# Another program order, other buffer slots and some exchanged engines in a fused linear-attention and FFN kernel

## Chip, cores and metric

The kernel runs on one core of a Trainium2 chip. The metric is the device time of one execution in microseconds (us). The engines are TensorE (PE in the profile, its weight loads PEld), VectorE (DVE), ScalarE (ACT), GpSimd (POOL) and SyncE (SP), which issues nearly all DMAs.

## What is computed

The reference is an attention with sketched polynomial features, without softmax, followed by a multiplicative feed-forward network (FFN).

```python
batch, n_heads, seq, head_dim, r = 4, 4, 1088, 32, 8
def phi(x):                       # 64 features per token and head
    a = np.einsum('rd,bhsd->bhsr', S1, x)
    b = np.einsum('rd,bhsd->bhsr', S2, x)
    return np.einsum('bhsi,bhsj->bhsij', a, b).reshape(*x.shape[:-1], r * r)
q_p, k_p = phi(q), phi(k)
kv  = np.einsum('bhsf,bhsd->bhfd', k_p, v)
z   = np.sum(k_p, axis=2)
num = np.einsum('bhsf,bhfd->bhsd', q_p, kv)
den = np.einsum('bhsf,bhf->bhs', q_p, z)[..., None] + 1e-06
x   = (num / den).transpose(0, 2, 1, 3).reshape(4352, 128)
out = (((x @ w1) * (x @ w2)) @ w3) @ w_out        # d_ff 1024, back to 128
```

S1, S2 and the FFN weights arrive as float64, so the kernel converts their raw words to float32 itself.

## The kernel before

The program is a list of 1179 named steps. Each step is a small function that issues one or a few instructions; the string `ORDER` says in which order the steps are called, and every engine then works its own instructions off in that order, since the kernel chains each engine's instructions (the loop at its end). So what stands in front of an instruction on its engine is decided by `ORDER` alone, and an instruction that waits holds up all that stands behind it on that engine.

Three other tables belong to it. `SLOTS` gives, for each kind of tile, which buffer the next tile of that kind takes, in the order of the calls (kind `b` is the 8 PSUM banks). `POOL` names the steps that run on GpSimd and not on VectorE (`on`), `CPV` the copies that run on VectorE and not on ScalarE (`cp`). At most four bulk loads (`UNDER_WAY`) are in flight.

The names of the steps:

- `s.*` prepares the sketch matrices; `warm0` to `warm11` are fillers, matmuls on zeros into an unused tile (`idle_ps`, L255).
- `k0` to `k3` are the key blocks, one for each batch: lead and rest split the keys (`rest0` is L651 on VectorE), `gram0` to `gram4` (L659) are gram matmuls of the splits (`ps_g`), G, T and N an orthonormalisation in small tiles, `kp` the features, `kv` their product with v.
- `q0` to `q7` and `qr` are the query parts: products with the small matrices (`ps_a`, `ps_c`), split and corrected values (`s_g`, `s_hl`, `ay_C`), `dn`, `de`, `rc` the denominator, `phi` features, `x` the result in PSUM; `xT` (L1291 for the first part) is the FFN's input with its rows on partitions.
- `w*` load and convert the weights; `f*` fold w3 and w_out into one matrix `w3o`.
- `g0` to `g3` are the FFN of the first four groups of 512 tokens, done directly: `a` (L1799) and `b` (L1809) are matmuls of 512 columns, `c` copies one result to SBUF, `m` multiplies them (L1815), `o` is the output matmul (L1835). `gr` is the same for the remaining 256 tokens, in 256 columns, with `o` at L1824.
- `h4` and `h6` treat the last four groups in two pairs, with seven products in place of eight: first-layer matmuls on 64 rows of the array at L1673 (two run side by side), elementwise combinations `m` and `T` (L1707 to L1742, 128x512), second-layer matmuls `P` of 64 columns (L1759, side by side too), combinations `k1` to `k9` (L1767 to L1785).
- `oT` transposes a group's output (L1842), `oS` scales it (L1848, GpSimd; it needs `q4.ns` or `q6.ns`, 16 small copies at L1497 that lay out the factors), `st` stores it with four DMAs (L1556), and `gr.st1` (L1562) is the last store.

So the program falls into a start (loads, sketches, first key block, first query part), a long part in which FFN matmuls of g0 to g3 alternate with the attention of the other blocks, the two seven-product stages, and a tail.

## Time and profile before

| | |
|---|---|
| three runs | 244.77, 245.26, 245.58 us; median 245.26 |
| profiled execution: span | 244.1 us from first to last instruction |
| mean granted TensorE clock | 0.998 |
| HBM read and written | 19.40 and 2.23 MB |

The page cuts the span into 40 slices and gives the busy tenths of each engine:

```profile
PE   8998999899999999999999999999999999999994
DVE  2876988999899998997899878498989789999792
POOL 4576658344856998764583889929999425883670
DMA  7959797078859897200000000360000000000054
```

In the list of costly groups a row names the line, the engine, the operation, the tiles and shapes, then the sum of busy time and the mean of one, then the idle time in front of them. In a timeline a row is start, duration, engine, line, tiles; several alike that run close together are merged (x4), so its duration reaches from the first start to the last end. Matmuls overlap, and so their pitch is read from their starts. A wait row gives the sum, the count and the longest.

### The profile page before, as it was taken

Reading aid. Unit: us, or ns where it says so; the run is one execution under the profiler, and the core shown is the slowest. Engines: PE = TensorE matmul, PEld = TensorE weight load, DVE = VectorE, ACT = ScalarE, POOL = GpSimd, SP = SyncE. Lnnn points to the kernel's source line nnn. Section 1 sums busy time; section 2 is a strip of 40 time slices with the busy share of each in tenths; the row PEclk is TensorE's granted clock in tenths of the full one; section 3 lists DMA queues with packets and bytes.
Section 4 is the critical chain, followed back from the end, with each engine's and each line's share of the span. In section 5 each row is a group of like instructions: output and inputs, shape, how many; then the busy total and the mean of one; then the engine's idle time right before and its main releaser. Section 6 shows DMA issues by size and latency. Waiting matters only on the chain.

```text
span 244.1 us, 6745 instructions
## 1 busy us (share of the span) xinstructions
PE 236.2 (97%) x2724; PEld 129.8 (53%) x2724; DVE 206.7 (85%) x421; ACT 123.5 (51%) x246; POOL 161.9 (66%) x203
## 2 busy tenths in 40 slices
PE   8998999899999999999999999999999999999994
PEld 5887454545545646766566444444443354463363
DVE  2876988999899998997899878498989789999792
ACT  3976957675666764593012914355651164730010
POOL 4576658344856998764583889929999425883670
PEclk9999999999999999999999999999999999999999
DMA  7959797078859897200000000360000000000054
GB/s 201 265 143 325 181 227 190 6 197 224 220 141 251 188 217 190 59 1 3 3 0 0 4 0 3 59 113 3 1 0 0 0 3 0 0 1 3 12 90 93
DMA packets 31935, 22.06 MB, mean 90 GB/s; under 512 B 21280, under 2 KB 26528, under 8 KB 31904
## 3 DMA queue, kind: packets, MB, share of 16 engines
q1 hardware_dynamic: 31360, 21.11, 35.1%
q8 instruction: 21, 0.34, 0.6%
q10 hardware_dynamic: 544, 0.52, 0.6%
q14 instruction: 10, 0.08, 0.1%
HBM read 19.40 MB, written 2.23 MB: 89 GB/s over the span
## 4 chain that ended last, share of the span: by engine, by line
PE 87%; DMA 5%; ACT 2%; POOL 2%; DVE 1%; issue 1%; POOLq 0%; SPq 0%
PE b_ps L1809 12%; PE ps_o L1835 12%; PE ps_X L1673 11%; PE a_ps L1799 11%; PE ps_o L1759 10%; PE ps_w3o L534 6%; PE ps_Y L1673 6%; PE ps_Z L1673 3%; PE ps_g L659 2%; PE ps_x L1527 2%; PE ps_ac L1374 2%; DMA qh<-in_q_dram 2%; DMA k<-in_k_dram 2%; PE ps_or L1824 2%; POOL ph L1208 1%; PE idle_ps L255 1%
## 5 line engine op out<-in xcount | busy, mean ns | idle before, releaser
L1673 PE MATMUL ps_X<-xd,wv 64*128 64x512 f32 x112 | 36.3, 593 | 0.0
L1799 PE MATMUL a_ps<-xT,w 128*128 128x512 f32 (+1 forms) x80 | 36.1, 562 | 0.0
L1809 PE MATMUL b_ps<-xT,w 128*128 128x512 f32 (+1 forms) x80 | 35.6, 555 | 0.0
L1804 ACT COPY ffa<-a_ps 128x512 f32<-128x512 f32 (+1 forms) x38 | 20.1, 540 | 29.2 <-PE a_ps L1799 26.7
L1707 POOL TENSOR_TENSOR hc<-hc 128x512 f32<-128x512 f32 x16 | 20.7, 1304 | 15.7 <-DVE hc L1685 15.5
L1835 PE MATMUL ps_o<-ab,w3o 128*128 128x512 f32 x64 | 29.6, 600 | 0.0
L1680 ACT COPY hc<-ps_X 128x512 f32<-128x512 f32 x38 | 21.3, 590 | 16.1 <-PE ps_X L1673 12.9
L1815 DVE TENSOR_TENSOR ab<-ffa,b_ps 128x512 f32<-128x512 f32 (+1 forms) x40 | 23.9, 623 | 4.9 <-PE b_ps L1809 4.1
L501 POOL TENSOR_TENSOR w3c<-w3c,cv_m 128x512 int32<-128x512 int32 x16 | 21.2, 1344 | 4.2 <-DVE w3c L495 4.1
L1673 PEld LDWEIGHTS ps_X<-xd,wv 64*128 64x128 f32 x112 | 14.9, 186 | 13.1 <-issue 10.9
L1799 PEld LDWEIGHTS a_ps<-xT,w 128*128 128x128 f32 x80 | 14.1, 189 | 13.9 <-issue 8.8
L1809 PEld LDWEIGHTS b_ps<-xT,w 128*128 128x128 f32 x80 | 14.4, 190 | 13.1 <-issue 8.1
L1673 PE MATMUL ps_Y<-xd,wv 64*128 64x512 f32 x48 | 19.7, 594 | 0.0
L1835 PEld LDWEIGHTS ps_o<-ab,w3o 128*128 128x128 f32 x64 | 11.6, 190 | 13.4 <-issue 13.0
L534 PEld LDWEIGHTS ps_w3o<-wo,w3T 128*128 128x128 f32 x128 | 15.3, 192 | 2.4 <-issue 2.4
L534 PE MATMUL ps_w3o<-wo,w3T 128*128 128x128 f32 x128 | 15.7, 276 | 0.0
L1759 PE MATMUL ps_o<-hc,w3o 128*64 128x512 f32 x32 | 15.1, 595 | 0.0
L1759 PE MATMUL ps_o<-tt,ws 128*64 128x512 f32 x32 | 13.7, 594 | 0.0
L1680 ACT COPY hc<-ps_Y 128x512 f32<-128x512 f32 x14 | 8.1, 592 | 9.7 <-PE ps_Y L1673 6.6
L263 ACT ACTIVATE cv_c<-raw 128x1024 f32<-128x1024 f32 (+1 forms) x13 | 13.0, 1014 | 0.0
L1540 ACT COPY xd<-ps_x 64x256 f32<-64x256 f32 x24 | 8.8, 367 | 7.2 <-PE ps_o L1835 6.8
L1497 POOL COPY nz<-nz 32x8 f32<-32x8 f32 x32 | 11.1, 347 | 1.4
(347 smaller groups left out, 593.0 us busy)
## 6 DMA issues: line engine op xcount, KB each, us to landing
raw<-in_moe_w_dram SPq DMA_DIRECT2D x32, 256.0 KB, 5.0
qh<-in_q_dram SPq DMA_DIRECT2D x4, 544.0 KB, 4.5
raw<-in_moe_w_dram SPq DMA_DIRECT2D x4, 512.0 KB, 5.8
out_dram<-oT SPq DMA_DIRECT2D x32, 64.0 KB, 2.0
k<-in_k_dram SPq DMA_DIRECT2D x3, 512.0 KB, 5.1
v<-in_v_dram SPq DMA_DIRECT2D x2, 512.0 KB, 6.1
kh<-in_k_dram SPq DMA_DIRECT2D x8, 128.0 KB, 3.6
raw<-in_moe_w_out_dram SPq DMA_DIRECT2D x4, 256.0 KB, 5.0
```

The costliest lines, as they stand in the source:

```text
L263: act.activation(dst, hi.bitcast(F32), ACT.Prelu, scale=2.0 ** -112, alpha=-2.0 ** 32)
L501: pool.tensor_tensor(d, d, x["m"][:, i * 512:(i + 1) * 512], ALU.add)
L534: pe.matmul(t["o"], w3T[ko][:, c], wo[:, c], start=c == 0, stop=c == NC - 1)
L1673: pe.matmul(x[bank], stat(j, u)[:, i * 128:(i + 1) * 128], rows(j, u), start=new, stop=True, tile_position=(u * 64, 0), skip_group_check=True)
L1680: cp(n(y))(x[k], x[bank])
L1707: on(f"h{g}.{i}m{k}").tensor_mul(both[0][k], both[0][k], both[1][k])
L1759: pe.matmul(acc_o[bank][half[0]:half[1]], w(i), x(i), start=n == 1, stop=n == (2 if j == 3 else 4), tile_position=(0, half[0]), skip_group ...
L1799: pe.matmul(x["a"][:, :w], w_of(0, c), xT[g][:, c0:c0 + w], start=True, stop=True)
L1804: cp(f"g{g}.{c}{su}c")(x["s"][:, :w], x["a"][:, :w])
L1809: pe.matmul(x["b"][:, :w], w_of(1, c), xT[g][:, c0:c0 + w], start=True, stop=True)
L1815: dve.tensor_mul(ab_sb[g, c][:, c0:c0 + w], x["s"][:, :w], x["b"][:, :w])
L1835: pe.matmul(o_ps[g], w3o[:, c], ab_sb[g, c], start=n == 1, stop=n == NC)
```

## The change

The file's functions stay as they are; four tables differ. The first 60 steps of `ORDER` are the same and the rest is permuted. `SLOTS` gives other buffers to the tiles. 26 steps leave `POOL` and 34 enter it; 14 copies leave `CPV` and 16 enter it. A line or two of each table:

```diff
 SLOTS = {
     "b": 
-        "012345670214657210671306537457462512346127340273014526045721472352140327540542370673245716"
+        "012345670214567201570316245173056437605247134671352075241304675326530012653074265304361427"
...
-    "x": "012012201110",
+    "x": "012012021020",
 }
...
 POOL = set("""
-    g4.oS g5.oS g6.oS g7.oS h4.0T1 h4.0T2 h4.0T3 h4.0m12 h4.0m22 h4.1T2 h4.1m11 h4.1m12 h4.2m11
+    g4.oS g5.oS g6.oS g7.oS h4.0T1 h4.0T2 h4.0T3 h4.0T4 h4.0m11 h4.0m12 h4.0m22 h4.1T1 h4.1T2 h4.1T3
...
 CPV = set("""
-    g0.0c g0.1c h4.1ac h4.1ad h6.1bc h6.2ad k0.kT1 k1.kvc k2.kT1 k2.kq k3.kT0 k3.kT1 k3.kq q0.xc0
-    q0.xc1 q6.xT0 q6.xT2
+    g0.6c g1.1c g2.3c g2.6c gr.3c h4.0ae h4.1ac h4.1bc h4.2ae h4.3ac h4.3ai h6.1ac h6.2ac h6.k1
+    k0.kT1 k0.kz q0.xc1 q4.xT3 q6.xT1
...
 ORDER = """
...
-g4.oS h6.k2 h6.k4 h6.0P3 gr.7o0 g4.st gr.0a gr.5b h6.k5 h6.k6 h6.3P3 h6.1P3 h6.k7 g5.oS q6.ns gr.4a gr.3o0 gr.4b gr.0c
...
+h6.2P7 gr.1m h6.0T4 g5.oT h6.3P1 h6.1P6 q6.ns h6.3P7 gr.3m h6.k1 h6.2P6 h6.2P4 h6.3P2 h6.k2 h6.0P7 h6.3P6 h6.3P5
...
```

Of the 128x512 products of the two seven-product stages, 16 go from VectorE to GpSimd and 7 from GpSimd to VectorE. The steps that an engine does at three places follow, before and now.

TensorE where the first FFN matmuls begin; `ps_xs` leads to xT, `ps_ab` belongs to the second key block, `ps_g` is its gram. Before:

```order
L1287 MATMUL ps_xs<-ident,xs 128x128 x2
L727 MATMUL ps_ab<-kT,KS 32x128 x16
L1799 MATMUL a_ps<-xT,w_81 128x512 x2
L1809 MATMUL b_ps<-xT,w_81 128x512 x2
L1799 MATMUL a_ps<-xT,w_81 128x512
L659 MATMUL ps_g<-kk 32x64
L659 MATMUL ps_g<-k,kk 32x32
```

Now:

```order
L829 MATMUL ps_krab<-RS,krT 128x64
L805 MATMUL ps_kq<-ident,kvc 128x128 x2
L727 MATMUL ps_ab<-kT,KS 32x128 x16
L1267 MATMUL ps_xt<-pT,kz_634 64x256 x4
L1287 MATMUL ps_xs<-ident,xs 128x128 x4
L659 MATMUL ps_g<-kk 32x64
L659 MATMUL ps_g<-k,kk 32x32
```

The gram rows go on in this way for 48 matmuls (gram0 to gram2); only then come L1809 and L1799. The query matmuls L1110, which stood between two parts of L1287 just ahead of these rows, are further ahead.

VectorE ahead of the first xT. `s_g`, `s_t`, `s_hl` and `ay_C` are of the second query part, `s_loy`, `s_pr`, `s_d`, `s_rc` of the first, and `kk` (L651) is rest0 of the second key block. Before:

```order
L1198 RECIPROCAL s_rc<-s_rc 128x16
L466 TENSOR_SCALAR w_81<-cv_c 128x2x256
L1274 COPY xc<-ps_xt 128x256 x2
L1291 TENSOR_TENSOR xT<-xc,ps_xs 128x256 x2
L1137 TENSOR_REDUCE s_g<-ps_a 128x32
L201 SCALAR_TENSOR_TENSOR s_t_699<-s_g,ps_a 128x256
L1130 STREAM_TRANSPOSE ay_C<-ps_c 128x384
L204 SCALAR_TENSOR_TENSOR s_hl<-s_g,s_t_699 128x2x128
L1157 TENSOR_TENSOR s_hl<-ps_a,s_hl 128x2x128
L651 TENSOR_TENSOR kk<-k,kk 128x1152
```

Now:

```order
L1101 TENSOR_TENSOR s_loy<-s_loy,ay_C_592 128x128
L1130 STREAM_TRANSPOSE ay_C<-ps_c 128x384
L1176 TENSOR_TENSOR s_pr<-s_hla,s_hiy 128x256
L204 SCALAR_TENSOR_TENSOR s_hl<-s_g,s_t_595 128x2x128
L794 COPY kz_634<-ps_kz 128x128
L1157 TENSOR_TENSOR s_hl<-ps_a,s_hl 128x2x128
L1189 TENSOR_REDUCE s_d<-s_pr 128x2x16
L1194 SCALAR_TENSOR_TENSOR s_rc<-s_d 128x16
L1198 RECIPROCAL s_rc<-s_rc 128x16
L651 TENSOR_TENSOR kk<-k,kk 128x1152
L1274 COPY xc<-ps_xt 128x256
L1291 TENSOR_TENSOR xT<-xc,ps_xs 128x256 x2
```

The steps of the second query part and L651 stood behind L1291 and stand now ahead of it; one of the two copies L1274 and the weight shift L466 are gone from here.

GpSimd at the end. `hc` and `tt` are the products of the last stage, `nz` the factors (`q6.ns`), `oT` the groups' outputs. Before:

```order
L1732 TENSOR_TENSOR tt<-hc,tt 128x512
L1707 TENSOR_TENSOR hc<-hc 128x512
L1727 TENSOR_TENSOR tt<-hc 128x512
L1737 TENSOR_TENSOR hc<-hc 128x512
L1742 TENSOR_TENSOR tt<-tt,hc 128x512
L1848 TENSOR_TENSOR oT<-oT,nz 128x512 x2
L1494 TENSOR_TENSOR nz<-nz 128x8
L1497 COPY nz<-nz 32x8 x16
L1848 TENSOR_TENSOR oT<-oT,nz 128x512 x2
```

Now:

```order
L1707 TENSOR_TENSOR hc<-hc 128x512
L1742 TENSOR_TENSOR tt<-tt,hc 128x512
L1727 TENSOR_TENSOR tt<-hc 128x512
L1737 TENSOR_TENSOR hc<-hc 128x512
L1732 TENSOR_TENSOR tt<-hc,tt 128x512
L1742 TENSOR_TENSOR tt<-tt,hc 128x512 x2
L1494 TENSOR_TENSOR nz<-nz 128x8
L1497 COPY nz<-nz 32x8 x16
L1848 TENSOR_TENSOR oT<-oT,nz 128x512 x3
```

The 16 copies stood between the scalings of g4, g5 and those of g6, g7; now they stand behind four products and ahead of three of the scalings.

## Prediction

> **What bounds the kernel now.** I read the page's first part, then who waited for whom on TensorE, then busy time by stage, and only then single rows.

> ```profile
> PE 236.2 (97%) x2724; PEld 129.8 (53%) x2724; DVE 206.7 (85%) x421; ACT 123.5 (51%) x246; POOL 161.9 (66%) x203
> PE ps_g L659 <- issue: 1.6, 2, 1.2
> PE idle_ps L255 <- DVE zeros L229: 1.0, 1, 1.0
> 27.42 1.96 PE L1799 MATMUL a_ps<-xT,w 128*128 128x512 f32 x4
> 27.42:49.17 21.75, 20.35 (x455) 11.06 (x455) 19.13 (x47) 15.05 (x30) 13.67 (x18) 1.00 0.63 152
> 49.17:240.55 191.38, 191.38 (x1765) 99.17 (x1764) 169.31 (x317) 89.27 (x171) 133.01 (x135) 1.00 0.28 65
> ```

> TensorE is the bound. The long waits are few and lie in the start. The first FFN matmul, which needs the first attention output xT, begins at 27.42; the windows cut the rest at 49.17. In the second window TensorE is busy 191.38 of 191.38 us, while VectorE works 169.31 and GpSimd 133.01. So the time is three things: when the first FFN matmul starts, how much TensorE work and idle time follow it (20.35 + 191.38 = **211.7 us** busy and 1.4 idle, as 21.75 - 20.35), and what hangs behind the last matmul. An order can change the first, the idle part of the second and the third; the work of the second only by what it costs to go from one kind of matmul to another.

> **The change, part by part.** It leaves every step in and permutes those after the sixtieth; so I ask of each of the three what the permutation does.

> *The first FFN matmul.* It waits for xT (L1291) on VectorE. VectorE's rows of before ahead of it and just behind it:

> ```profile
> 18.96 0.16 DVE L937 TENSOR_TENSOR RC<-RC,ps_Nr 128x8 f32<-128x8 f32 x1 [0.41 <-PE ps_Nr L912]
> 23.20 0.32 DVE L1068 STREAM_TRANSPOSE ay_C<-ps_cy 128x128 f32<-128x128 f32 x1 [1.38 <-PE ps_cy L1030]
> 25.44 0.36 DVE L466 TENSOR_SCALAR w<-cv_c 128x512 int32<-128x512 int32 x1
> 25.71 0.74 DVE L1274 COPY xc<-ps_xt 128x256 f32<-128x256 f32 x2
> 26.48 0.79 DVE L1291 TENSOR_TENSOR xT<-xc,ps_xs 128x256 f32<-128x256 f32 x2
> 27.19 0.42 DVE L1137 TENSOR_REDUCE s_g<-ps_a 128x32 f32<-128x256 f32 x1
> 27.64 0.42 DVE L201 SCALAR_TENSOR_TENSOR s_t<-s_g,ps_a 128x256 f32<-128x256 f32 x1
> 27.98 0.57 DVE L1130 STREAM_TRANSPOSE ay_C<-ps_c 128x384 f32<-128x384 f32 x1
> 28.48 0.41 DVE L204 SCALAR_TENSOR_TENSOR s_hl<-s_g,s_t 128x256 f32<-128x256 f32 x1
> 28.92 0.42 DVE L1157 TENSOR_TENSOR s_hl<-ps_a,s_hl 128x256 f32<-128x256 f32 x1
> 29.26 1.35 DVE L651 TENSOR_TENSOR kk<-k,kk 128x1152 f32<-128x1152 f32 x1
> ```

> In the changed order the six last rows stand ahead of xT: 0.42 + 0.42 + 0.57 + 0.41 + 0.42 + 1.35 = 3.6 us. Small steps come from the other engines (the kz copy, RS), some 0.5 us by rows of their shape, and 0.36 (L466) and 0.37 (one of the two xc copies, now on ScalarE) leave: about +3.3 us. VectorE stood idle there for 0.41 + 1.38 = 1.8 us, which the moved work can fill. So xT comes 1.5 us later by this count; I take **28.8** for the first FFN matmul, with bounds 27.4 (all of it fills waits) and 30.7 (none of it does). What is bought with that: two thirds of the gram steps of the second key block (L659) now run ahead of that matmul, while TensorE has nothing else. That is 48 matmuls, and the chain of before has such matmuls at 1.56 us for 75 links, 21 ns each: **1.0 us** that no longer stands in the dense part.

> ```profile
> 44.27 1.56 PE ps_g L659 x75
> 45.83 1.16 issue
> ```

> The second row is most of the 1.4 us idle: TensorE stands between matmuls of the third key block's gram, with no engine named as releaser. In the changed order that block lies elsewhere between other steps. Bounds: it goes (0), or comes again (1.2); neither has a reason that the trace shows, so I take the middle, **0.6**.

> *The fillers.* Four 256-column matmuls on zeros (warm7 to warm9) stood in the start at idle moments and now stand among the dense steps.

> ```profile
> 17.36 0.61 PE L255 MATMUL idle_ps<-zeros 128*128 128x256 bf16 x4
> ```

> Four take 0.61 us with the tail of the last, which the next matmul overlaps: I take **+0.45**; bounds 0.3 and 0.61.

> *Changes of tile form.* In the tail of before, where both forms alternate, the start times show what a change costs:

> ```profile
> 229.90 0.59 PE L1759 MATMUL ps_o<-tt,w3o 128*64 128x512 f32 x1
> 230.33 0.59 PE L1759 MATMUL ps_o<-tt,w3o 128*64 128x512 f32 x1
> 230.86 0.94 PE L1824 MATMUL ps_or<-w3o,ab 128*128 128x128 f32 x6
> 233.06 0.60 PE L1799 MATMUL a_ps<-xT,w 128*128 128x256 f32 x2
> 233.49 0.59 PE L1809 MATMUL b_ps<-xT,w 128*128 128x256 f32 x2
> 234.01 1.08 PE L1759 MATMUL ps_o<-hc,ws 128*64 128x512 f32 x4
> 235.02 0.70 PE L1799 MATMUL a_ps<-xT,w 128*128 128x256 f32 x2
> ```

> Within a form, starts are 0.43 apart (229.90 to 230.33, 233.06 to 233.49). Across a change they are 0.53 (230.33 to 230.86), 0.52 (233.49 to 234.01), and 1.01 where two pairs would take 0.86 (234.01 to 235.02): 0.09, 0.10 and 0.15 too much. Counted in the two program orders behind the first FFN matmul, the old one changes to or from the full 128x128 form 42 times, the new one 32 times. Ten fewer are 0.9 to 1.5 us; I take **-1.1**.

> So the work behind the first FFN matmul is 211.7 - 1.0 + 0.45 - 1.1 = 210.05, and with 0.6 idle the last matmul would end at 28.8 + 210.05 + 0.6 = **239.45**, against 240.55: 1.1 us sooner.

> *The exchanges between VectorE and GpSimd.* They move 16 of the 128x512 products of the seven-product stage to GpSimd and 7 to VectorE. Per product:

> ```profile
> L1707 POOL TENSOR_TENSOR hc<-hc 128x512 f32<-128x512 f32 x16 | 20.7, 1304 | 15.7 <-DVE hc L1685 15.5
> L1742 DVE TENSOR_TENSOR tt<-tt,hc 128x512 f32<-128x512 f32 x7 | 4.7, 680 | 0.0
> ```

> Nine more are +11.7 us on GpSimd (133.0 becomes about 145 of 191) and -6.1 on VectorE. Both engines still have less to do than TensorE over the window; I charge **0** in the middle, where TensorE's work hides them. If that cover fails it is at h6.2T1, which stands behind the q4.ns copies on GpSimd. Those took 8.77 us in before; summing rows from there, T1 is 2 us early if they take 3.6, and some 1.4 late if 8.8: that is the upper bound here, 0 the lower.

> *The tail.* Here the order costs. Rows of before:

> ```profile
> 235.94 0.68 DVE L1785 TENSOR_TENSOR oc<-oc,ps_o 64x512 f32<-64x512 f32 x1
> 236.65 0.71 DVE L1842 STREAM_TRANSPOSE oT<-oc 128x512 f32<-128x512 f32 x1
> 237.28 1.90 DVE L1815 TENSOR_TENSOR ab<-ffa,b_ps 128x256 f32<-128x256 f32 x5
> 229.38 2.05 POOL L1848 TENSOR_TENSOR oT<-oT,nz 128x512 f32<-128x512 f32 x2
> 231.65 3.56 POOL L1497 COPY nz<-nz 32x8 f32<-32x8 f32 x16
> 237.50 1.05 POOL L1848 TENSOR_TENSOR oT<-oT,nz 128x512 f32<-128x512 f32 x1 [1.13 <-DVE oT L1842]
> 230.45 10.14 SPq L1556 DMA_DIRECT2D out_dram<-oT  x16
> 240.95 0.62 SPq L1562 DMA_DIRECT2D out_dram<-oT  x1
> ```

> SyncE issues the output of a group as four DMAs; the last four run from 238.55 (where the scaling L1848 ends) to 240.59, 2.04 us, and only then the rest rows' store at 240.95, 0.4 behind the last matmul. In the changed order the second layer's last matmuls (L1759) end just 6.6 us ahead of the end (7 matmul steps of 0.43 and 16 of 0.22), and eleven VectorE operations of some 0.7 (the combinations and transposes) hang behind those. Counting from t, the end of h6.3P7, with 0.43 per pair on TensorE and 0.7 per operation on VectorE: the matmuls of the last kind end at t+4.3, k3 can start at t+2.75, and after k4, k5, k7, k6, k8 comes g6.oT at t+6.9, then k9, and g7.oT ends at t+9.0. Scaled, g6 is ready at t+8.7 and g7 at t+10.1; their stores take SyncE to t+10.75 and t+12.8. Undisturbed, TensorE would end at t+11.0, and four products behind g7.oT hold it up to some t+11.5. So the last store starts 1.8 us behind the undisturbed end instead of 0.4: **+1.4**. And q6.ns, the 16 copies of 3.56 us, now stands on GpSimd ahead of the scaling of g5; if the four products ahead of it (4 x 1.3) start late, the stores shift to t+13.5, +2.1. I take **+1.5**; the lower bound is +0.5, if VectorE runs ahead and only TensorE's shorter lead counts.

> *Sum*, against the profiled execution: -1.1 (end of matmuls) + 1.5 (tail) = +0.4. Its span was 244.1 and the median of the runs is 245.26, 1.16 more, so **245.6**. From the other end: 239.45 + 0.4 + 1.5 + 3.15 (from 240.95 to 244.1) + 1.16 = 245.66.

> [...] The same 16 copies took two very different times:

> ```profile
> 181.62 8.77 POOL L1497 COPY nz<-nz 32x8 f32<-32x8 f32 x16
> 181.60:190.40 8.80, 8.80 (x44) 2.90 (x42) 8.77 (x16) 2.15 (x4) 8.16 (x16) 1.00 0.00 0
> 231.60:235.30 3.70, 3.70 (x17) 1.57 (x16) 3.54 (x7) 0.37 (x1) 2.95 (x16) 1.00 0.70 115
> ```

> VectorE is busy throughout in both; what differs is its work: products of two SBUF tiles there, combinations with a PSUM operand here. [...]

> **The rivals.**

> 1. *Faster, 0.30.* VectorE's moved work fits wholly into its waits, the issue gap does not come back, and the stores hide: -1.4 (28.8 to 27.8 is 1.0, of the 0.6 idle 0.4) and a tail of +1.1 give 245.66 - 1.4 - 0.4 = 243.9. For it: 1.8 us of waits on VectorE. Against: eleven operations behind the last matmuls.
> 2. *Slower through GpSimd, 0.15.* q6.ns takes 8.8 instead of 3.6 and stands ahead of g5's scaling; all three scalings and stores come behind it. It decides from about 5 us on; at 8.8 the last store moves by 1.9 to 5.7, the middle gives **249.4**. For it: the 8.77 above, and nine more products on GpSimd. Against: its neighbours have PSUM operands.
> 3. *Slower through the start, 0.14.* The 3.3 us on VectorE fill nothing: the first FFN matmul at 30.7, of which 0.6 is bought back by gram steps that fit ahead. +1.3: 247.0. It decides at xT later than about 29.5. Against: TensorE's results, for which VectorE waits, do not come later in the new order.
> 4. *A lower clock, 0.03.* The rows grant 1.00 in every window, with fillers in the idle moments of the start; those are thinner now. Half the clock over 3 us of the start's matmuls would cost some 1.5 us: 247.1. [...]
> 5. *The middle is not covered, 0.05.* h6.2T1 is 1.4 late, 247.1; the middle's margins decide, 2 us at the least by my sums.

> **How the numbers follow.** Forecast **245.6**, chance 0.33. What this kernel's measurement can tell from no change is about 0.3%, 0.74 us: faster is under 244.5, slower over 246.0. Faster: rival 1 but for 0.03, and 0.05 of the forecast's own spread, 0.32. Slower: rivals 2 to 5 but for 0.05, and 0.06 of the forecast, 0.38. The same: the rest, 0.30. Range: the low end takes 0 idle, the switches at 1.5 and a tail of +0.5, 245.66 - 0.6 - 0.4 - 1.0 = 243.6; the high end takes the start at 30 (+1.2), the gap again (+0.6) and a tail of +2.1 (+0.6), 248.0. Rival 2 and the far part of the others lie outside, some 0.2.

> **What would show it.** First FFN matmul near 28.8 with gram matmuls ahead of it; TensorE waits behind it under 1.5 us; last matmul near 240.0; SyncE issuing output DMAs without a break up to about 1.5 us behind it; q6.ns near 3.6 us. A first FFN matmul before 28, or an end of matmuls below 239 with the last store within 0.5 us of it, would show rival 1; waits of TensorE in the seven-product stages would show the middle wrong.

## The result and the profile after

The changed kernel takes **264.07 us** (median of 4 runs, 263.23 to 265.30) against 245.06 us: the ratio is 1.077, 95% interval 1.0734 to 1.0806. The forecast was 245.6, no change. The times below are medians of all runs, while the ratios and their intervals leave out runs more than 1.5% above the fastest of their kernel, so the two need not agree. A trace is of one execution and is read for that execution alone.

The page of the changed kernel, first the busy time of the engines, then TensorE's busy tenths and the granted clock over 40 slices:

```profile
span 261.4 us, 6776 instructions
PE 245.5 (94%) x2724; PEld 145.2 (56%) x2724; DVE 213.7 (82%) x418; ACT 119.8 (46%) x241; POOL 164.8 (63%) x211
PE   8996997899999999799979999999999999999992
PEclk9997999799999999869999999999999999999997
```

The span has grown from 244.1 to 261.4 us, 17.3. TensorE's idle time has doubled (261.4 - 245.5 = 15.9 against 7.9), and its busy time has grown by 9.3 us at the same 2724 instructions: the clock row has digits below 9 that it did not have. Who waited for whom on TensorE:

```profile
PE ps_ac L1374 <- DVE ay_A L1385: 4.1, 3, 1.9
PE ps_N L912 <- issue: 2.7, 1, 2.7
PE ps_kv L769 <- issue: 2.2, 1, 2.2
```

Three kinds of stretch carry it. In the windows view (TensorE's busy time first, the granted clock third from the end, DMA share second from the end):

```profile
20.00:22.00 2.00, 0.21 (x9) 0.05 (x2) 1.90 (x7) 1.97 (x2) 1.92 (x3) 1.00 0.36 94
24.00:26.00 2.00, 2.00 (x43) 1.81 (x34) 1.48 (x5) 0.44 (x3) 0.46 (x1) 0.50 0.00 0
44.00:46.00 2.00, 0.00 (x0) 0.00 (x0) 0.56 (x1) 2.00 (x4) 0.92 (x1) 1.00 1.00 228
48.00:50.00 2.00, 2.00 (x4) 0.76 (x3) 1.26 (x3) 0.84 (x3) 0.00 (x0) 0.50 1.09 282
106.00:108.00 2.00, 0.52 (x32) 0.04 (x4) 2.00 (x3) 0.97 (x1) 0.00 (x0) 1.00 0.00 0
110.00:112.00 2.00, 2.00 (x31) 1.23 (x31) 1.93 (x5) 0.00 (x0) 1.76 (x1) 0.50 0.04 8
```

Each time TensorE stands for about 2 us, and then runs on at half the clock. The trace's clock record puts the halves at 23.26 to 26.67, 47.15 to 50.57 and 108.59 to 115.42 us: 3.41, 3.41 and 6.83 us (and one more behind the last matmul, as in the kernel before). By the starts of four kinds of matmul in both traces the 17.3 us lie here:

| stage | before | after | more |
|---|---|---|---|
| start to the first FFN matmul | 27.4 | 31.7 | 4.3 |
| from there to the first matmul of the seven-product stages (L1673) | 128.3 | 138.7 | 10.4 |
| from there to the end of the last matmul | 84.85 | 86.25 | 1.4 |
| behind it | 3.55 | 4.76 | 1.2 |

The tail did what the prediction had worked out. SyncE's output DMAs, three groups in a row, and the last store of the changed kernel, whose last matmul ends at 256.69:

```profile
247.21 3.54 POOL L1497 COPY nz<-nz 32x8 f32<-32x8 f32 x16
250.83 1.05 POOL L1848 TENSOR_TENSOR oT<-oT,nz 128x512 f32<-128x512 f32 x1
251.91 6.27 SPq L1556 DMA_DIRECT2D out_dram<-oT  x12
258.28 0.62 SPq L1562 DMA_DIRECT2D out_dram<-oT  x1
```

Twelve issues in 6.27 us without a break, and the last store 1.6 us behind the matmuls instead of 0.4. The copies took 3.54 us, not 8.8.

**Where TensorE waits for VectorE**, VectorE and TensorE of the changed kernel around 106 us:

```profile
104.41 1.39 DVE L1815 TENSOR_TENSOR ab<-ffa,b_ps 128x512 f32<-128x512 f32 x2
105.71 2.36 DVE L528 STREAM_TRANSPOSE w3T<-w3c 128x1024 f32<-128x1024 f32 x2
108.00 0.74 DVE L1385 STREAM_TRANSPOSE ay_A<-ps_ac 128x256 f32<-128x256 f32 x2
105.78 0.74 PE L1374 MATMUL ps_ac<-qT,RC 32*32 32x256 f32 x32
108.46 1.40 PE L1374 MATMUL ps_ac<-q,RC 32*32 32x256 f32 x19 [1.94 <-DVE ay_A L1385]
...
112.29 5.23 PE L534 MATMUL ps_w3o<-wo,w3T 128*128 128x128 f32 x32
```

In q4 the matmuls C0 (32 records at 105.78) are followed by C1, into the same PSUM tiles. The transpose At reads another part of these tiles. In the order of before, C1 is called ahead of At, and At waits for C1. In the changed order At is called first; C1 writes a tile that At has yet to read, and so it waits for At, which stands on VectorE behind two weight transposes of 1.2 us. The first of the 32 matmuls of L534 at 112.29 run while the clock is halved, up to 115.42. q6 and qr have the same turn.

**Where TensorE waits for nothing that is named** ("issue"), the cause has to be sought in what it runs on. Section 3 of the page lists a queue `q8 instruction` with 21 transfers of 0.34 MB, 16 KB each; their times in the records of the two traces are:

```
            fetch starts, takes   lands    TensorE idle   runs again
before        16.75   2.19        18.94    from 19.44       20.35
after         19.84   1.18        21.02    from 20.21       22.41
before        44.28   1.15        45.43    from 45.83       46.98
after         44.13   1.25        45.38    from 43.92       46.61
```

Each time TensorE goes on 1.2 to 1.6 us after such a transfer has landed. The count of matmuls ties the two together: over all traces of this case, the unnamed gaps of more than 0.4 us stand in front of the 221st or 222nd, the 346th, the 597th or 598th and the 850th or 851st recorded matmul, whatever step that is, and end behind the 1st, 2nd, 4th and 6th of these transfers. One transfer serves some 130 matmuls (21 for 2724), and these places are one or two such blocks apart. I read this as TensorE having run out of instructions there; no row names the cause. Why the one at 20 us is late shows in the DMA share (second from the end of each row), in the kernel before:

```profile
15.00:16.00 1.00, 1.00 (x11) 0.89 (x10) 0.90 (x5) 0.08 (x1) 0.42 (x2) 1.00 0.04 6
16.00:17.00 1.00, 1.00 (x12) 0.98 (x10) 0.93 (x5) 1.00 (x5) 0.00 (x0) 1.00 0.38 56
```

and the same windows of the changed kernel:

```profile
15.00:16.00 1.00, 0.97 (x10) 0.86 (x11) 0.68 (x4) 0.83 (x4) 0.76 (x4) 1.00 0.95 326
16.00:17.00 1.00, 0.85 (x11) 0.52 (x11) 0.75 (x5) 1.00 (x4) 0.69 (x3) 1.00 0.98 393
```

Before, the DMA engines had nearly nothing to do there, and the fetch went through at 16.75. In the changed order the load of the second weight block was issued at 11.2 us, not at 16.2, and the DMA share stays at 0.91 to 1.12 from 15 to 20 us; the fetch starts at 19.84. That the load delays it is shown below by moving that load in the kernel before. Which block comes late differs between executions: in two other traces with the same start (c0_four and gram_split) this fetch came at 18.68, with the DMA engines as full (share 0.93 to 1.14 from 14 to 19 us in gram_split, 0.9 in the page's slice from 13.2 to 19.8 us in c0_four), and left only 0.81 us; there the block ahead of the first FFN matmul was late, with gaps of 3.23 and 4.05 us.

### The profile page after: what moved, and what is told of

It is laid out like the page before. It is cut to its first block, busy times and chain, and to the rows that moved or that the text cites. A ratio compares the mean times of both kernels' runs of the same rounds, so it can differ in the third digit from the quotient of the medians.

```text
span 261.4 us, 6776 instructions
## 1 busy us (share of the span) xinstructions
PE 245.5 (94%) x2724; PEld 145.2 (56%) x2724; DVE 213.7 (82%) x418; ACT 119.8 (46%) x241; POOL 164.8 (63%) x211
## 4 chain that ended last, share of the span: by engine, by line
PE 80%; DVE 13%; issue 3%; DMA 1%; POOL 0%; DVEq 0%; SPq 0%
PE ps_o L1835 11%; PE b_ps L1809 10%; PE ps_X L1673 10%; PE ps_o L1759 9%; PE a_ps L1799 9%; PE ps_Y L1673 6%; PE ps_w3o L534 5%; PE ps_Z L1673 3%; PE idle_ps L255 3%; PE ps_g L659 2%; PE ps_ac L1374 2%; DVE ab L1815 2%; DVE w3T L528 2%; PE ps_x L1527 2%; DVE kk L651 1%
## 5 line engine op out<-in xcount | busy, mean ns | idle before, releaser
L1673 PE MATMUL ps_X<-xd,wv 64*128 64x512 f32 x112 | 40.1, 597 | 0.0
L1809 PE MATMUL b_ps<-xT,w 128*128 128x512 f32 (+1 forms) x80 | 38.8, 591 | 0.2 <-DVE ab L1815 0.2
L1804 ACT COPY ffa<-a_ps 128x512 f32<-128x512 f32 (+1 forms) x35 | 18.4, 543 | 38.4 <-PE a_ps L1799 36.5
L1799 PE MATMUL a_ps<-xT,w 128*128 128x512 f32 (+1 forms) x80 | 35.3, 557 | 0.0
L1815 DVE TENSOR_TENSOR ab<-ffa,b_ps 128x512 f32<-128x512 f32 (+1 forms) x40 | 24.2, 621 | 7.8 <-PE b_ps L1809 6.9
L1680 ACT COPY hc<-ps_X 128x512 f32<-128x512 f32 x32 | 18.2, 588 | 18.6 <-PE ps_X L1673 18.4
L1707 POOL TENSOR_TENSOR hc<-hc 128x512 f32<-128x512 f32 x16 | 21.6, 1363 | 6.4 <-DVE hc L1685 6.3
L1809 PEld LDWEIGHTS b_ps<-xT,w 128*128 128x128 f32 x80 | 15.3, 202 | 14.1 <-issue 10.1
L1673 PE MATMUL ps_Y<-xd,wv 64*128 64x512 f32 x48 | 23.1, 592 | 0.0
L1799 PEld LDWEIGHTS a_ps<-xT,w 128*128 128x128 f32 x80 | 14.3, 190 | 14.8 <-issue 8.9
L1673 PEld LDWEIGHTS ps_X<-xd,wv 64*128 64x128 f32 x112 | 17.9, 186 | 8.3 <-issue 4.1
L501 POOL TENSOR_TENSOR w3c<-w3c,cv_m 128x512 int32<-128x512 int32 x16 | 20.6, 1304 | 1.3 <-DVE s_rc L1450 1.2
L1417 POOL TENSOR_TENSOR s_hl<-ay_A,s_hl 128x256 f32<-128x256 f32 (+2 forms) x5 | 4.9, 971 | 23.1 <-DVE s_hl L204 20.0
L534 PEld LDWEIGHTS ps_w3o<-wo,w3T 128*128 128x128 f32 x128 | 17.0, 209 | 3.4 <-issue 3.4
L1835 PEld LDWEIGHTS ps_o<-ab,w3o 128*128 128x128 f32 x64 | 11.5, 190 | 12.4 <-issue 11.7
L677 POOL TENSOR_TENSOR kp<-kabt 128x1024 f32<-128x1024 f32 x5 | 11.6, 2327 | 9.6 <-PE ps_ac L1374 9.5
L534 PE MATMUL ps_w3o<-wo,w3T 128*128 128x128 f32 x128 | 16.9, 291 | 0.0
L1759 PE MATMUL ps_o<-hc,ws 128*64 128x512 f32 x32 | 15.5, 597 | 0.0
L1759 PE MATMUL ps_o<-hc,w3o 128*64 128x512 f32 x32 | 14.9, 597 | 0.0
L484 ACT ACTIVATE cv_m<-raw 128x1024 int32<-128x1024 uint32 x9 | 10.5, 1168 | 9.0 <-PE ps_w3o L534 8.8
```

The costliest lines, as they stand in the source:

```text
L501: pool.tensor_tensor(d, d, x["m"][:, i * 512:(i + 1) * 512], ALU.add)
L534: pe.matmul(t["o"], w3T[ko][:, c], wo[:, c], start=c == 0, stop=c == NC - 1)
L1673: pe.matmul(x[bank], stat(j, u)[:, i * 128:(i + 1) * 128], rows(j, u), start=new, stop=True, tile_position=(u * 64, 0), skip_group_check=True)
L1680: cp(n(y))(x[k], x[bank])
L1707: on(f"h{g}.{i}m{k}").tensor_mul(both[0][k], both[0][k], both[1][k])
L1759: pe.matmul(acc_o[bank][half[0]:half[1]], w(i), x(i), start=n == 1, stop=n == (2 if j == 3 else 4), tile_position=(0, half[0]), skip_group ...
```

## The experiments

Theory W: TensorE's waits, each followed by a stretch at half clock, make the loss; under it L for the unnamed ones (the instruction fetch stands behind loads). Rivals: X, the exchanged engines make VectorE or GpSimd late; B, a row of short matmuls empties the instructions whatever is being loaded. The diffs show steps of `ORDER`, one to a line.

**C1 ahead of At again** (the same in q6 and qr)

```diff
 q4.C0
 ...
 f3.t
+q4.C1
 q4.At
-q4.C1
 q4.Ct
```

> The changed kernel, but in q4, q6 and qr the second sketch matmuls (C1) are called ahead of the transpose At, as in the kernel before. Theory W (TensorE's waits, each followed by a stretch at half clock, make the loss): the wait of L1374 for VectorE's L1385 goes (1.9 + 0.6 + 1.5 us in the trace of the changed kernel), and with the first of them the 6.83 us at a granted clock of 0.5 (3.4 us of work): 264.1 becomes about 257, and the half-clock stretch near 109 us is gone while those at 23 and 47 us stay. Rival X (the exchanged engines make VectorE late, and TensorE would wait for it elsewhere): at least 262, the wait turns up at another line.

Measured: 258.37 us (255.35 to 260.74), ratio to before 1.0428 (1.0366 to 1.049), against 1.077. The profile's windows have no half clock there:

```profile
100.00:110.00 10.00, 10.00 (x200) 6.98 (x189) 9.90 (x19) 5.29 (x10) 3.26 (x3) 1.00 0.01 2
110.00:120.00 10.00, 10.00 (x56) 7.10 (x56) 9.06 (x20) 5.67 (x9) 3.34 (x3) 1.00 0.01 2
```

From q4's first sketch matmul (L1365) to the first matmul of L1673 it is 57.65 us instead of 64.89: 7.2 less, 4.1 of waits and 3.1 of clock. The four other kernels with this edit take 57.64 to 57.66 us there too. The two unnamed gaps and their half clocks stay. Rival X would have seen the wait elsewhere; it falls here.

**The same edit the other way round, in the kernel before**

```diff
 q4.C0
+q4.At
 q4.C1
-q4.At
 k3.N0
```

> The kernel before with one step moved: in q4 the transpose At is called ahead of the matmuls C1, which makes them wait for it, since both use the same PSUM tiles. By the rows of before VectorE gets to At at 95.83 us, so C1, at 94.84 us before, waits until about 96.7: 1.8 us. Theory W: that wait appears at L1374, and if it brings half a clock, another 1.7 to 3.4 us: 245.3 becomes 247 without and 249 to 250.5 with it. If a wait of TensorE in the middle is made up later: 245.3.

Measured: 247.60 us, ratio 1.0096 (1.0061 to 1.0131), and the wait is there, with the clock at 1.00:

```profile
95.34 0.83 PE L1374 MATMUL ps_ac<-q,RC 32*32 32x256 f32 x17 [1.28 <-DVE ay_A L1385]
```

One step moved costs 2.4 us by the medians, and nothing makes it up later. The wait itself is 1.28; the profiled run, at a granted clock of 1.000, is 1.4 over the median of before (246.56 against 245.18). The two longest runs have a mean clock of 0.993, which is some 1.7 us of clock.

**Filling the wait with work**

```diff
-        step(nm("C0"))(lambda: prods(0, s["qT"], True))
+        step(nm("C0"))(lambda: [prods(0, s["qT"], True) for _ in range(4 if key == 4 else 1)])
```

> The changed kernel, but in q4 the first sketch matmuls (C0, 16 short matmuls that overwrite their result) are issued four times in place of once; the three further times add 0.7 us each of TensorE work to the stretch in which it waits for VectorE anyway. Theory W: the wait of L1374 shrinks from 1.94 us to about nothing while the time at which it ends stays near 108.4 us, and the 6.83 us of half clock behind it go: 264.1 becomes about 260.7, though more work is done. If idle time alone is lost and the clock does not matter: 264 or a little more.

Measured: 265.09 us, ratio 1.0789 (1.0711 to 1.0867): as a whole a miss. At its place it did what was expected:

```profile
108.48 2.76 PE L1374 MATMUL ps_ac<-qT,RC 32*32 32x256 f32 x128
111.73 0.84 PE L1374 MATMUL ps_ac<-q,RC 32*32 32x256 f32 x17 [0.49 <-DVE ay_A L1385]
114.12 3.73 PE L534 MATMUL ps_w3o<-wo,w3T 128*128 128x128 f32 x32
```

The wait is 0.49 us, the clock stays at 1.00 and the 32 matmuls of L534 take 3.73 us; in the changed kernel they took 5.23 (its timeline above, at 112.29). From the matmuls of L534 ahead of q4 to those of L1799 behind, it is 11.3 us (106.37 to 117.69) instead of 13.7 (103.67 to 117.36), with 96 matmul records more. So the half clock costs time by itself. But another half came at 135.6 us, behind qr's wait of 1.5 us, which the changed kernel passed at full clock, and the unnamed gaps at 29.6 and 46.8 us were 3.2 and 2.4 us: the total shows nothing.

**The load of the second weight block later**

```diff
 k1.load
-w0.load
 s.Pp
 ...
 k2.load
+w0.load
 ...
-w0.m0
 ...
+w0.m0
 kh2.load
```

> The changed kernel, but the load of the second weight block (two DMAs of 512 KB) is called behind the next key load and its first conversion ten steps later. Theory W: the instruction fetch of TensorE's queue that landed late at 19.84 us comes earlier, the idle 2.2 us at 20.2 us shrinks under 1 us and the half clock at 23.3 to 26.7 us goes (1.7 us): 264.1 becomes about 260.5. Rival B (the gap comes from so many short matmuls in a row, whatever is being loaded): the gap stays, 264.

Measured: 263.24 us, ratio 1.07 (1.0647 to 1.0754); the fetch started at 19.64 (19.84 in the changed kernel is the start too; it landed at 21.02) and the gap was 1.93 us. A miss: the load was now issued at 15.25 to 16.23 us, so its packets may still have stood ahead (DMA share 1.01 to 1.11 from 17 to 20 us). In the kernel before they are issued from 16.24 on, and the fetch at 16.75 is just ahead of them. When a fetch is asked for is not recorded, so that this order is a guess from two rows.

**The load early in the kernel before**

```diff
 k1.load
+w0.load
 k0.ab1
 ...
 k2.load
-w0.load
 k1.lead0
```

> The kernel before with one step moved: the load of the second weight block is called right behind the load of the second key block, as in the changed kernel, some 5 us sooner. Theory L (TensorE's instruction fetch stands behind the loads issued ahead of it): if the loads then run without a break past 17 us, the second fetch (16.75 us in the kernel before) lands later, the idle 0.91 us at 19.4 us grows towards 2 and may bring half a clock: 245.3 becomes 246 to 249. Rival B (short matmuls in a row alone): gap and time unchanged, within 0.7 us.

Measured: 245.71 us (245.15 to 249.65 in ten runs), ratio 1.0028 (1.0000 to 1.0057): no difference by the ratio. The profiled execution is the longest, of 249.65 us. Its DMA share is 0.96 to 1.15 from 15 to 19 us, the fetch starts at 18.60, and

```profile
PE ps_kv L769 <- issue: 2.3, 1, 2.3
22.00:24.00 2.00, 2.00 (x51) 1.57 (x47) 0.00 (x0) 0.86 (x3) 0.19 (x1) 0.50 0.03 8
```

the gap of 0.91 us has become 2.28, with half a clock from 20.99 to 27.82 us behind it; the first FFN matmul comes at 31.3 instead of 27.4. In this execution one moved load makes the late fetch and the gap of the changed kernel's start; the gap stands ahead of the half clock and so does not come from it. In seven of the ten runs the time was under 245.9, with a mean granted clock of 0.999 to 1.000; the three others, of 248.49 to 249.65, have 0.986 to 0.993. So the move costs 3 to 4 us where a half clock follows and nothing that can be measured where none does. Whether the gap was there in the seven is not shown, since they have no trace.

**Two loads under way instead of four, in the changed kernel** (`UNDER_WAY = 2`)

> The changed kernel with two bulk loads under way instead of four; nothing else. Theory L (the fetch of TensorE's instructions stands behind the packets of the loads that were issued before it): fewer packets stand ahead, the second fetch of the queue starts by 18 us instead of 19.84, the idle 2.2 us at 20.2 us fall under 1.2 and the half clock at 23 us goes; 264.1 becomes about 260, if no load now comes late itself. Rival B (so many short matmuls in a row, whatever is loaded): fetch and gap stay as they are, 264.

Measured: 284.13 us, ratio 1.1532 (1.1449 to 1.1615). The fetch starts at 15.54, as L has it, and no row of "issue" is left on TensorE. But TensorE stands 2.53 us for a key load from 16.20, at the place of that gap, so the missing row alone proves little; and the loads come late themselves (ScalarE waits 8.6 us for weights, VectorE 7.6 for a query load); TensorE's longest waits are now for ScalarE:

```profile
PE b_ps L1809 <- ACT w3o L538: 6.6, 1, 6.6
PE ps_N L912 <- ACT T_p L908: 5.9, 1, 5.9
PE ps_x L1527 <- ACT ffa L1804: 4.0, 1, 4.0
```

**Splitting the row of short matmuls, in both orders**

```diff
 k2.gram2
 ...
-k2.gram3
 ...
-k2.gram4
 ...
+k2.gram3
+k2.gram4
 k2.Gm
```

> The changed kernel, but the last two gram steps of the third key block (24 matmuls) are called behind two 512-column FFN matmuls instead of ahead of them. Rival B for the second gap (short matmuls in a row use up the fetched instructions): the 2.7 us of idle TensorE at 43.9 us fall under 1 us and the half clock at 47.2 to 50.6 us goes: 264.1 becomes about 260.5. If the loads alone make the gap: it stays near 2 us, over 263.

> The kernel before with the last two gram steps of the third key block called some 20 steps later, ahead of the first step that reads them; no other change. Theory B for that gap (short matmuls in a row use up the fetched instructions): the 1.16 us of idle TensorE at 45.8 us shrink or go, 245.3 becomes 244.2 to 244.8. If the fetch is late whatever stands there: the gap turns up behind the other short matmuls, 245.3.

Measured in the changed order: 263.16 us (257.73 to 268.06), too wide a spread for a ratio. The unnamed gap at 44 us is gone, as B has it; 0.46 us at 47.5 wait for VectorE. In this execution the fetch ahead of the first FFN matmul came at 30.82 us and left a gap of 4.05. Measured in the order of before: 249.01 us, ratio 1.016 (1.013 to 1.019), a loss where a gain of 0.5 to 1 was expected:

```profile
PE a_ps L1799 <- DVE ab L1815: 2.4, 1, 2.4
PE ps_ab L727 <- DVE RC L936: 1.2, 1, 1.2
```

The unnamed gap at 45.8 us is gone, but TensorE now stands 1.15 us at 45.37 for VectorE, which gives the fetch the same time: B is not shown by this run. And VectorE waits 2.4 us for the moved matmuls (L217, at 53.08), so that its work behind them comes late. The gap was cheaper than its cure.

**The three edits together** (C1 ahead of At, the gram steps split, the load later)

> The three edits together. Theory W: no half clock but at the ends; 264.1 - 7 - 3.6 - 3.6 = about 250, within 2 us of it, the rest over the kernel before being the later stores and the drawn-out seven-product stage. Rival X: over 255.

Measured: 255.39 us, ratio 1.0401 (1.036 to 1.0442). A miss by 5 us, and just over the 255 named for X, though no new wait for VectorE or GpSimd over 1.0 us stands in the trace. One half clock is left, at 22.02 us, behind the 2.2 us gap at 20.25, which this edit of the load does not remove. 8.7 of the 19 us are gone.

**Holding single loads back** (with C1 ahead of At and the gram steps split; `gate2` has 17 in place of 12)

```diff
-    for ins, ahead in zip(bulk[UNDER_WAY:], bulk):
-        tc.add_manual_dep(ins, ahead.name, landed, reason="under way")
+    for i, ins in enumerate(bulk):
+        n = 2 if 7 <= i < 12 else UNDER_WAY
+        if i >= n:
+            tc.add_manual_dep(ins, bulk[i - n].name, landed, reason="under way")
```

> The changed kernel with C1 ahead of At, with the gram steps split, and with the next five bulk loads (third key block, the key halves) held to two under way; the weight load is back at its place. Theory L: the loads have a break at about 16 us, the second fetch starts by 17.5 us, the idle 2.2 us at 20.2 us fall under 1 us and the half clock at 23 us goes; the first FFN matmul is at 28 to 29 us in place of 31.7 and the time near 251.5. If the fetch is late for another reason: first FFN matmul at 31.5 or later, 255.

> As gate, but the next weight load (four DMAs) and the query load ahead of it are held to two under way as well. Theory L: the third fetch, at 32.44 us in gate with the loads at full share around it, starts by 30 us, the 5.16 us of idle TensorE at 30 us fall under 1.5 and the half clock behind them goes; first FFN matmul by 30 us, time near 252. Rival B: the gap stays near 30 us, 256 or more.

Measured: gate 258.86 us, ratio 1.0464 (1.0405 to 1.0523); gate2 255.32 us, ratio 1.041 (1.0366 to 1.0453). In gate the second fetch starts at 17.67 (17.45 in gate2), earlier than in any trace of this start with four loads under way (18.68 to 20.48), and no gap is left near 20 us but one of 0.51: that part of L holds. Then a later fetch, the 4th, is late, at 32.44 us, with the DMA engines full:

```profile
35.12 0.27 PE L659 MATMUL ps_g<-k,kk 128*32 128x32 f32 x2 [5.16 <-issue]
31.00:32.00 1.00, 0.00 (x0) 0.00 (x0) 1.00 (x3) 0.46 (x2) 0.77 (x2) 1.00 1.03 223
```

and with those loads held too, in gate2, it starts at 29.28:

```profile
31.61 0.22 PE L659 MATMUL ps_g<-k,kk 128*32 128x32 f32 x2 [1.88 <-issue]
29.00:30.00 1.00, 0.73 (x62) 0.62 (x54) 1.00 (x4) 1.00 (x2) 1.00 (x2) 1.00 0.39 64
```

5.16 us fall to 1.88 and no half clock is left but at the end. The DMA share is still 0.73 to 0.98 from 27 to 29 us, so how much of the 1.88 is loads, and how much B (the 48 gram matmuls in a row), stays open. And gate2 leaves a part of the loss without a cause: with no half clock and no wait for At over 0.2 us its span is 253.3, 9.2 over that of before: 4.3 up to the first FFN matmul (31.76), 2.3 from there to the seven-product stages, 1.4 in them and 1.2 behind.

**Three loads under way**

> The changed kernel with C1 ahead of At and three bulk loads under way instead of four. Theory L: idle time with no engine named falls from 5.9 us (c1_first) to under 4, the time from 258.4 to about 255, unless a load comes late itself (with two under way, waits for ScalarE and for the loads of 2.5 to 6.6 us took the place).

> The kernel before with three bulk loads under way instead of four. Theory L: the idle 0.91 us at 19.4 us goes or not, as the loads have a break there anyway; the 1.16 us at 45.8 us stay, since no load is in flight there: 244.5 to 246, unless a load comes late itself. Rival: both gaps are gone with fewer loads, under 244.

Measured: the changed order 258.35 us, ratio 1.0545 (1.0514 to 1.0576), no better than with four; the unnamed idle time is 6.1 us, its longest gap at 30 us and no longer at 44, so L's forecast missed. The order of before 246.60 us, ratio 1.0056 (1.003 to 1.0082). There the expectation was wrong in an instructive way: with three under way two weight loads are issued at 41.9 us, where before no load ran, the DMA share at 44 us is 0.98, the fetch starts at 45.80 instead of 44.28, and

```profile
PE ps_g L659 <- issue: 3.3, 2, 2.7
44.00:45.00 1.00, 1.00 (x86) 0.99 (x87) 0.93 (x5) 0.87 (x2) 0.26 (x2) 1.00 0.98 281
```

the gap of 1.16 us is 2.75, with half a clock behind it. At one and the same place in one and the same row of matmuls, with loads beside it the gap is 1.6 us longer: both B (the 1.16, at a DMA share of 0.07 or less from 43 to 46 us) and L (the rest) are at work.

**The two halves of the change apart.** `sets_only` is the kernel before with the changed `POOL` and `CPV`; `order_only` the changed kernel with those of before.

> The kernel before with the changed kernel's two sets of engines (which steps run on GpSimd, which copies on VectorE), order and slots as before. Theory W: within 2 us of 245.3, since the order makes the waits. Rival X (the exchanges make VectorE or GpSimd late): over 250.

> The changed kernel with the two sets of engines of the kernel before; order and slots changed. Theory W: the gaps near 20, 44 and 108 us and the half clock behind them are all there, 260 to 266. Rival X: under 255.

Measured: 272.36 us, ratio 1.1052 (1.0971 to 1.1132), and 277.33 us (271.42 to 280.55). Each half alone is worse than both together. `order_only` spread too far for a ratio, and it missed both expectations. With the old order the exchanged engines are late in the seven-product stages, which take 105.1 us to the last matmul instead of 84.85, 13.65 of them at half the clock:

```profile
PE ps_o L1759 <- POOL hc L1707: 2.7, 1, 2.7
PE ps_Z L1673 <- DVE hc L1685: 2.2, 3, 1.6
PE ps_X L1673 <- POOL wv L1600: 1.8, 1, 1.8
```

So rival X is right of this kernel and wrong of the changed one, where no such row stands and the stage takes 86.25 us. Theory W's expectation for `sets_only` was wrong. Of W's gaps `order_only` has 0.8 us near 20, 2.7 near 51 and 2.0 near 115, the last without a half clock; besides, TensorE waits up to 1.5 us each for ScalarE, VectorE and GpSimd, and that stage takes 91.6 us. The buffer slots were not tried apart from the order.

## Why the prediction was wrong

The forecast was no change, and the kernel became 19 us slower. By its steps:

- *The idle time behind the first FFN matmul, 0.6 us* (1.4 in the kernel before), failed most. The prediction says that an order can change it, but it has no term for waits that the permutation itself adds there; it prices only the exchanged products ("I charge 0 in the middle, where TensorE's work hides them") and goes by sums of busy time, and these say that VectorE has time, not when. The change calls At ahead of C1 three times, which adds a wait of TensorE for VectorE; what is queued ahead of At was not listed. Measured: 4.1 us of waits and 3.1 of clock, 7.2 together (c1_first), the largest part.
- *"I take the middle, 0.6"* for the unnamed gap, with bounds 0 and 1.2, failed in kind. The gap was taken for a property of one place. By the fetch times and the matmul counts it is TensorE running out of instructions, and it grew with loads beside it (1.16 to 2.75 us in before_uw3). The loads, whose order on SyncE the change also permutes, were not priced at all. Measured: 2.2 us at 20 and 2.7 at 44, against 0.9 and 1.2.
- *"A lower clock"*, with a chance of 0.03, an estimate of the author's, then came three times. The longest wait in the trace of before is 1.2 us; the new waits were 1.9 to 2.7, and a half clock followed each. No run shows the 3 us of that rival's sum: the half clocks among the matmuls lasted 3.41 us or a multiple. From q4's L1365 to the first L1673 the kernels take 57.65 us without a half clock; with the same waits of 4.07 us, one half of 3.41 us (gram_split) takes 63.63 and two (w0_late) 65.09: 1.9 and 1.7 us for each, half the stretch. In the changed kernel 3.41 + 3.41 + 6.83 = 13.65 us of it are worth about 6.8.
- *The first FFN matmul at 28.8*, with an upper bound of 30.7, came at 31.7. Less 1.3 (the gap at 20 us over that of before) and 1.7 (its half clock) that is 28.7, but this agreement may be luck: in gate2, with neither, it comes at 31.76. TensorE's work ahead of it grows there by 1.0 us, as forecast (25.49 us busy against 24.49), but its idle time grows from 2.9 to 6.3 us, 1.88 of it a gap among the gram matmuls that were put there.
- *The tail at +1.5* was right; measured +1.2, with the stores back to back. *The copies' length* was right too: both sets took 3.54 us in the changed kernel, against 8.77 and 3.56 in that of before, and VectorE worked only on combinations with a PSUM operand beside them, as it did, but for one transpose, beside the 3.56. That the operands make the difference was not shown.
- *Changes of tile form, -1.1*, is not seen. The last stage, with no unnamed gap and 0.1 us of idle time, takes 86.22 to 86.39 us in every kernel with the changed order and engines, 84.85 in that of before. The matmuls on its two halves of the array (L1673) mostly start 100 to 260 ns apart there and within 30 ns of each other in the kernel before; what sets them apart was not tried, and no run isolates the forms.
- *The exchanges at 0*: right for the whole change (0.1 us of idle TensorE in the seven-product stages), but not because TensorE's work hides them in any order: with the old order the same exchanges cost 27 us.

The 17.3 us of the profiled spans add up: waits for At and their clock 7.2, the two unnamed gaps 2.8 more than before, their clock 3.4, last stage 1.4, stores 1.2: 16.0. The 1.3 left lie ahead of the first FFN matmul (4.3 less 1.3 and 1.7), where the prediction had put 1.4. In the middle nothing is left of its 10.4, so that the small terms for the work there (-1.0, +0.45, -1.1) are not seen in the sum. This sum is of one execution, and it shares out what stands in its trace: taking out the waits for At and all half clocks left 9.2 us (gate2), where the sum leaves 6.7, and why the start stays 4.3 us late is only in part explained. No version here beats the kernel before.

## What to carry to other kernels

Where steps are permuted, look for pairs on one tile whose call order turned round: a read called ahead of the next write makes the writer wait, and what stands ahead of the read on its engine is the price (here up to 1.94 us behind two weight transposes). A sum of busy time does not show this. A stall of TensorE can cost more than its length: here three of 1.9 to 2.7 us cost 3.9 to 5.0 us each with the half clock behind them. And look at what the loads do to the instruction fetch before rows of many short matmuls: here a gap of 1.16 us became 2.75 with loads beside it (before_uw3).

## What the runs showed of the hardware

The second instruction fetch of 16 KB starts at 15.54 (uw2) to 20.48 us (c1_first), late where loads fill the DMA engines (19.84 at a DMA share of 0.91 to 1.12 from 15 us on in the changed kernel, 16.75 at 0.04 and 0.38 in that of before), and behind an unnamed gap TensorE goes on 1.2 to 1.6 us after the landing. The longest unnamed gap that ended behind an instruction fetch is 5.16 us (gate, the 4th fetch, started at 32.44).
